# Fused attention and two MoE layers on one core: four of a slot's seven second-layer sums made by a ScalarE copy and an accumulating transfer

## Chip, cores and metric

The kernel runs on one core of a Trainium2 chip. The metric is device microseconds of one execution. One execution was also taken by the hardware profiler; all rows below come from it.

## The reference, cut to what matters

```python
# attention: 8 batches, 8 heads, 576 tokens, head size 64
kv = einsum('bhsd,bhse->bhde', k, v)
o  = einsum('bhsd,bhde->bhse', q, kv)
o  = o / sqrt(mean(o*o) + 1e-6) * g_norm          # -> x: 4608 tokens x 512
# first MoE layer (512 -> 2048 -> 512)
h = x @ w_in;  g = max(h, 0)**2;   x = g @ w_out
# second MoE layer (512 -> 2048 -> 512)
h = x @ w_in;  g = h * cos(h);     out = g @ w_out
```

All arrays are float32. A float32 product is made of three float32r matmuls on a high and a low part of each operand (high by high, high by low, low by high).

## The kernel before, in words

The 4608 tokens are worked in big tiles of 1024 tokens, in two halves of `ht` = 512; the last tile has 512 tokens, `ht` = 256. The part of the kernel that matters here walks 30 slots `(m, t, q)`: layer m, tile t, and a share q of the hidden units. The second layer (m = 1) has five tiles of four slots each, q = 0 to 3. A slot makes a 2 by 2 block product in two steps with seven block products each (Strassen's scheme in Winograd's form) in place of eight: `first_product` (x by w_in, into the PSUM tiles FA and FB), then a chain of ScalarE and VectorE operations for h*cos(h) (`cos_1` to `cos_5`) and block differences (`s_block`), then `second_product` (g by w_out, into the PSUM tiles SA and SB). The last slot of a tile, q = 3, makes its second step with `second` and `drain`, in the ordinary way, and stores the result to `out`.

The two steps are woven together on TensorE: while slot k makes its first products, the second products of slot k - 1.25 are issued between them. A product of the first step has 12 matmuls, one of the second step has 24 in a full tile (12 in the last tile). The time of one product of each is called a phase here; a slot has seven.

The second products come in the order `S_ORDER = (0, 2, 3, 4, 5, 1, 6)` and alternate between SA and SB. For four of them a product starts a bank anew or goes on adding in it, so each bank must have been read before the product after next begins. After the last matmul of a product `drain_product` reads the bank. The partial sums of a tile are four SBUF tiles of 128 x 1024 float32 (`sums`), kept over the tile's four slots. At q = 0 the products 0, 2, 3 and 6 start their sum with a ScalarE copy (L695); in all other cases VectorE adds the bank to the sum (L698).

`SUM_OF` says which sum a product goes to: 0 and 1 to (0,0), 2 and 5 to (1,1), 3 and 4 to (0,1), 6 to (1,0).

Weights come from DRAM, one transfer of 512 KB for each product (`load_wi`, L476, and `load_ws`, L481), issued on SP's queue. They share 16 buffers (`w_p`) with the four sums, so a load waits on SP until an earlier product has set a buffer free. `conv_p` is a pool of two buffers of 4 KB per partition with the tag "raw"; it serves the conversion of weights, which is over before the second products of the second layer begin. GpSimd's queue (POOL) issues no transfer in this part of the kernel; its only ones are 16 stores of 144 KB in the attention part (L354).

Each engine runs its instructions in the order in which they were issued.

Of the kernel before, what the change touches and what calls it, by code (L numbers as in the profile page):

```python
# [8 lines left out]
F32 = mybir.dt.float32  # L9
# [4 lines left out]
ALU = mybir.AluOpType  # L14
PSUM = bass.MemoryType.PSUM

P = 128
# [5 lines left out]
def kernel(  # L23
# [15 lines left out]
    nc = tc.nc  # L39
# [25 lines left out]
    conv_p = ctx.enter_context(tc.tile_pool(name="conv", bufs=2, side="left"))  # L65
# [356 lines left out]
    slots = [(m, t, q) for m in range(2) for t in range(len(TILES)) for q in groups_of[m]]  # L422
    ORDER = (0, 1, 3, 2, 5, 4, 6)
    W_OF = (0, 1, 3, 4, 6, 5, 2)
    BLOCKS = {(0, 0): 2, (1, 1): 5, (0, 1): 6, (1, 0): 7}
    S_ORDER = (0, 2, 3, 4, 5, 1, 6)
    xb, wi, wo, kept, hs, ys, sums, quads = {}, {}, {}, {}, {}, {}, {}, {}

    def big(pool, dtype, name, ht):
# [145 lines left out]
    def units(k):  # L575
        m, t, q = slots[k]
        half = TILES[t][1] // P if m else NKC
        return [(j, i) for j in (1, 0) for i in range(half)]
# [75 lines left out]
    def blocks_of(t, x, m=1):  # L654
        if m == 0:
            return x[:, :, :TILES[t][1]]
        return x.rearrange("p c n -> p (c n)").rearrange("p (b n) -> p b n", n=2 * P)[:, :TILES[t][1] // P]

    def s_bank(k, i):
        return psum[("SA", "SB")[(k + (i in (1, 2, 4))) % 2]]  # L660

    def second_product(k, i):
        m, t, q = slots[k]
        ps = blocks_of(t, s_bank(k, i), m)
        w, g = wo.pop((k, i)), gs.pop((k, i))
        nb = TILES[t][1] // P if m else 2
        for b in range(nb):
            n = 0
            for pp in range(2):
                for x, y in ((0, 0), (0, 1), (1, 0)):  # L670
                    if m == 0:
                        lhs, rhs = w[:, x, pp, b, :], g[y][:, pp, :]
                    else:
                        lhs, rhs = g[y][:, pp, b * P:(b + 1) * P], w[:, x, pp, :, :].rearrange("p i n -> p (i n)")
                    nc.tensor.matmul(  # L675
                        ps[:, b, :],
                        lhs,
                        rhs,
                        start=(i in (0, 1, 2) and n == 0 and (m == 0 or b % 2 == 0)),
                        stop=(n == 5),  # L680
                        skip_group_check=True,
                    )
                    n += 1
                    if n == 6 and b == nb - 1:
                        drain_product(k, i)
                    yield
# [3 lines left out]
    def drain_product(k, i):  # L690
        m, t, q = slots[k]
        ps, (d, j) = blocks_of(t, s_bank(k, i), m), SUM_OF[i]
        if q == 0 and m and i in (0, 2, 3, 6):
            sums[m, t, d, j] = e = w_p.tile([P, 2, 512], F32, tag="w", name="sum")
            nc.scalar.copy(out=blocks_of(t, e), in_=ps)  # L695
        else:
            e = blocks_of(t, sums[m, t, d, j], m)
            nc.vector.tensor_tensor(out=e, in0=ps, in1=e, op=ALU.add)  # L698


    chunks = [(t, f) for t in range(NTILE) for f in range(NH)]
# [5 lines left out]
    def at(n, fn, *a):  # L707
        jobs.append((n, len(jobs), fn, a))

    def pos(slot):  # L710
        return nA0 + slot + 0.002
# [67 lines left out]
    for k, (m, t, q) in enumerate(slots):  # L779
# [7 lines left out]
        if (m, q) in seven:  # L787
            for f, i in enumerate(S_ORDER):
                at(pos(k + LAG2 + (f - 2.7) * PH), load_ws, k, i)
# [54 lines left out]
    def run_slots():  # L844
# [9 lines left out]
            for k in range(len(slots))  # L854
            for i in (S_ORDER if slots[k][0::2] in seven else range(len(units(k)) // 4))
        ]
# [99 lines left out]
```

## Time and profile before

| | |
|---|---|
| median of 3 runs | 1594.78 us |
| lowest, highest | 1592.71, 1594.97 us |
| the profiled execution | 1593.87 us |
| its span, first to last instruction | 1592.1 us |
| TensorE busy, share of the span | 1555.1 us, 98% |
| VectorE busy | 1273.3 us, 80% |
| ScalarE busy | 992.7 us, 62% |
| GpSimd busy | 60.8 us, 4% |
| mean granted TensorE clock | 0.994 |

Times in the rows are microseconds from the start of the span. PE is TensorE's matmuls, PEld its weight loads, DVE VectorE, ACT ScalarE, POOL GpSimd, SP SyncE; a q behind a name is the engine's own instruction queue. L698 is line 698 of the kernel. "sum<-SA,sum" names the tile written and the tiles read.

### The profile page before, as it was taken

What the parts mean: (1) busy time and instruction counts of PE and PEld (TensorE: products, weight loads), DVE (VectorE), ACT (ScalarE), POOL (GpSimd) and SP (SyncE); (2) the same over time, 40 slices, a digit from 0 to 9 for tenths busy, and PEclk for the clock granted to TensorE, in tenths of its full rate; (3) what the DMA queues carried; (4) which work ended last, traced back from release to release, by engine and by line L of the source; (5) the groups of instructions that cost most, each with busy time, mean ns of one, the idle gap of its engine ahead of it and who ended that gap; (6) DMA issues with size and microseconds to landing.
All of it is one profiled execution on the core that took longest, in us unless ns stands there. A gap on an engine that the chain in (4) does not pass through costs nothing.

```text
span 1592.1 us, 23679 instructions
## 1 busy us (share of the span) xinstructions
PE 1555.1 (98%) x8840; PEld 1322.0 (83%) x8840; DVE 1273.3 (80%) x1724; ACT 992.7 (62%) x1422; POOL 60.8 (4%) x58
## 2 busy tenths in 40 slices
PE   5999999999999999999999999999999999999998
PEld 4777777778887778888888899889988998899897
DVE  7967767787766898989867789868986898689786
ACT  5977767784434666556646666666666666666664
POOL 1100112111100000000000000000000000000000
PEclk8999999999999999999999999999999999999999
DMA  9855876665568989898988856565656565656684
GB/s 316 279 168 159 256 238 223 200 207 184 164 214 274 318 283 352 304 353 292 351 311 333 286 177 212 180 244 172 212 187 237 172 213 180 229 174 206 214 338 191
DMA packets 214545, 382.20 MB, mean 240 GB/s; under 512 B 17312, under 2 KB 140704, under 8 KB 214432
## 3 DMA queue, kind: packets, MB, share of 16 engines
q1 hardware_dynamic: 213664, 378.34, 71.0%
q0 software_dynamic: 768, 2.36, 0.4%
q8 instruction: 70, 1.15, 0.3%
q14 instruction: 43, 0.35, 0.1%
HBM read 301.99 MB, written 78.64 MB: 239 GB/s over the span
## 4 chain that ended last, share of the span: by engine, by line
PE 87%; DVE 6%; DMA 3%; ACT 3%; issue 1%; SPq 0%; POOL 0%; DVEq 0%; ACTq 0%
PE FA L502 15%; PE FB L502 15%; PE SA L675 11%; PE SB L675 10%; PE acc L415 10%; PE l L378 8%; PE SA L604 6%; PE SB L604 6%; PE o L378 1%; PE ss L378 1%; DMA q<-in_qT 1%; PE o L257 1%; DMA x_d<-xo 1%; PE l L257 0%; DVE raw L173 0%
## 5 line engine op out<-in xcount | busy, mean ns | idle before, releaser
L502 PE MATMUL FA<-xh,wi 128*128 128x512 f32 (+1 forms) x840 | 304.0, 371 | 4.7 <-DVE h L526 1.7
L502 PE MATMUL FB<-xh,wi 128*128 128x512 f32 (+1 forms) x840 | 301.7, 369 | 0.0
L675 PE MATMUL SA<-ws,gh 128*128 128x256 f32 x792 | 197.0, 280 | 0.0
L675 PE MATMUL SB<-ws,gh 128*128 128x256 f32 x720 | 180.1, 280 | 0.0
L502 PEld LDWEIGHTS FA<-xh,wi 128*128 128x128 f32 x840 | 158.3, 189 | 20.8 <-DVE h L526 2.1
L502 PEld LDWEIGHTS FB<-xh,wi 128*128 128x128 f32 x840 | 157.7, 188 | 13.5
L675 PEld LDWEIGHTS SA<-ws,gh 128*128 128x128 f32 x792 | 147.8, 188 | 14.6 <-issue 0.2
L675 PEld LDWEIGHTS SB<-ws,gh 128*128 128x128 f32 x720 | 134.8, 188 | 13.6
L561 DVE SCALAR_TENSOR_TENSOR y<-y,h 128x1024 f32<-128x1024 f32 (+1 forms) x80 | 89.2, 1115 | 46.7 <-ACT y L557 46.7
L543 ACT ACTIVATE y<-h,zerob 128x1024 int32<-128x1024 f32 (+1 forms) x80 | 85.1, 1063 | 64.9 <-DVE h L522 64.9
L553 ACT ACTIVATE y<-y 128x1024 f32<-128x1024 f32 (+1 forms) x80 | 78.0, 976 | 75.8 <-DVE y L547 75.3
L415 PE MATMUL acc<-gh,wh 128*128 128x512 f32 x288 | 114.3, 398 | 0.0
L415 PE MATMUL acc<-gl,wh 128*128 128x512 f32 x288 | 113.5, 394 | 0.0
L415 PE MATMUL acc<-gh,wl 128*128 128x512 f32 x288 | 113.1, 393 | 0.0
L675 PE MATMUL SA<-ws,gl 128*128 128x256 f32 x396 | 111.0, 280 | 0.0
L502 PE MATMUL FB<-xl,wi 128*128 128x512 f32 (+1 forms) x300 | 110.9, 370 | 0.0
L502 PE MATMUL FA<-xl,wi 128*128 128x512 f32 (+1 forms) x300 | 110.8, 369 | 0.0
L652 DVE TENSOR_TENSOR gl<-y,gh 128x1024 fp32r<-128x1024 f32 (+1 forms) x75 | 83.5, 1114 | 30.0 <-ACT gh L651 30.0
L675 PE MATMUL SB<-ws,gl 128*128 128x256 f32 x360 | 100.9, 280 | 0.0
L378 PE MATMUL l<-xh,wh 128*128 128x512 f32 x240 | 96.5, 402 | 1.7 <-ACT xh L347 0.8
L378 PE MATMUL l<-xl,wh 128*128 128x512 f32 x240 | 94.9, 396 | 0.0
L378 PE MATMUL l<-xh,wl 128*128 128x512 f32 x240 | 94.4, 393 | 0.0
(190 smaller groups left out, 3859.8 us busy)
## 6 DMA issues: line engine op xcount, KB each, us to landing
wi<-wi_d SPq DMA_DIRECT2D x210, 512.0 KB, 5.1
ws<-ws_d SPq DMA_DIRECT2D x140, 512.0 KB, 5.3
wo<-wo_d SPq DMA_DIRECT2D x40, 512.0 KB, 5.2
kvld<-in_kv SPq DMA_DIRECT2D x32, 512.0 KB, 6.3
wi_d<-wh SPq DMA_DIRECT2D x24, 448.0 KB, 3.5
wi_d<-raw SPq DMA_DIRECT2D x24, 448.0 KB, 3.8
raw<-in_wA SPq DMA_DIRECT2D x20, 512.0 KB, 6.0
q<-in_qT SPq DMA_DIRECT2D x32, 288.0 KB, 4.0
```

Source lines behind the costliest of these rows:

```text
L257: nc.tensor.matmul(kv_ps[b][r, p, r], t[:n, 0, head], t[:n, 1, head], start=(c == 0 and p == 0), stop=(c == NSC - 1), skip_group_check=True,)
L378: nc.tensor.matmul(ps, a[:, 0, cs], m[:], start=(c == 0 and k == 0), stop=(c == NKC - 1 and k == 2))
L415: nc.tensor.matmul(o, a[:, cs], m[:], start=(f == 0 and n == 0), stop=(f == NH - 1 and n == 2), skip_group_check=True)
L502: nc.tensor.matmul(ps[:, pp, :], a, b, start=(i in (0, 1, 2) and n == 0), stop=(n == 5), skip_group_check=True)
L543: nc.scalar.activation(out=y.bitcast(I32), in_=hs[k, b], func=AF.Identity, bias=zerob)
L553: nc.scalar.activation(out=y, in_=y, func=AF.Sin, scale=math.pi)
L561: nc.vector.scalar_tensor_tensor(out=y, in0=y, scalar=-2.0 * math.pi, in1=hs.pop((k, b)), op0=ALU.add, op1=ALU.mult)
L604: nc.tensor.matmul(ps, lhs, rhs, start=(a == 0 and (x, y) == (0, 0)), stop=last, skip_group_check=True)
L652: nc.vector.tensor_tensor(out=l, in0=src, in1=as32(h), op=ALU.subtract)
L675: nc.tensor.matmul(ps[:, b, :], lhs, rhs, start=(i in (0, 1, 2) and n == 0 and (m == 0 or b % 2 == 0)), stop=(n == 5), skip_group_check=True,)
```

## The change

For the second layer, the four products 4, 5, 1 and 6 are no longer added to their sum by VectorE. ScalarE copies the bank to an SBUF tile `part` (a buffer of `conv_p`), and a transfer on GpSimd's queue adds `part` to the sum in SBUF. Where product 6 starts its sum (q = 0), its copy stays as it was. The first layer and the products 0, 2 and 3 are as before. The last condition (`k < len(slots) - 1`) is always true, since the last slot doesn't come here.

```diff
     S_ORDER = (0, 2, 3, 4, 5, 1, 6)
+    BY_DMA = (4, 5, 1, 6)
...
         else:
             e = blocks_of(t, sums[m, t, d, j], m)
-            nc.vector.tensor_tensor(out=e, in0=ps, in1=e, op=ALU.add)
+            if m and i in BY_DMA and k < len(slots) - 1:
+                part = blocks_of(t, conv_p.tile([P, 2, 512], F32, tag="raw", name="part"))
+                nc.scalar.copy(out=part, in_=ps)
+                nc.gpsimd.dma_start(out=e, in_=part, accum_op=ALU.add)
+            else:
+                nc.vector.tensor_tensor(out=e, in0=ps, in1=e, op=ALU.add)
```

## Rows read from the trace of the kernel before

**Rows 1.** The page, busy time of each engine, share of the span, instructions.
```profile
PE 1555.1 (98%) x8840; PEld 1322.0 (83%) x8840; DVE 1273.3 (80%) x1724; ACT 992.7 (62%) x1422; POOL 60.8 (4%) x58
```
**Rows 2.** Windows: stretch, length, then PE, PEld, DVE, ACT, POOL, clock, DMA, GB/s.
```profile
900.00:1592.00 692.00, 686.44 (x4239) 616.42 (x4237) 564.38 (x554) 434.75 (x474) 0.00 (x0) 1.00 0.62 211
...
1060.00:1100.00 40.00, 40.00 (x259) 36.33 (x258) 29.67 (x26) 26.88 (x28) 0.00 (x0) 1.00 0.65 224
1100.00:1150.00 50.00, 50.00 (x323) 45.36 (x322) 44.54 (x40) 32.26 (x33) 0.00 (x0) 1.00 0.65 207
...
1530.00:1540.00 10.00, 10.00 (x86) 10.00 (x85) 8.73 (x15) 7.28 (x13) 0.00 (x0) 1.00 1.03 418
...
1560.00:1570.00 10.00, 10.00 (x86) 10.00 (x85) 8.96 (x16) 6.38 (x11) 0.00 (x0) 1.00 0.83 335
1570.00:1580.00 10.00, 9.17 (x61) 8.28 (x61) 8.48 (x15) 7.68 (x13) 0.00 (x0) 1.00 0.00 0
```
**Rows 3.** Waits of PE from 900 to the end: total, times, longest.
```profile
PE SA L604 <- ACT y L557: 0.8, 1, 0.8
```
**Rows 4.** Lines 698 (first two) and 695, second layer: duration ns min/median/max, forms.
```profile
L698 DVE TENSOR_TENSOR sum<-SB,sum x45: 681/1217/1225, 917.1 to 1574.5; 128x1024 f32<-128x1024 f32 x36, 128x512 f32<-128x512 f32 x9
L698 DVE TENSOR_TENSOR sum<-SA,sum x40: 682/1217/1225, 922.8 to 1575.3; 128x1024 f32<-128x1024 f32 x32, 128x512 f32<-128x512 f32 x8
...
L695 ACT COPY sum<-SA x15: 578/1013/1017, 900.3 to 1537.8; 128x1024 f32<-128x1024 f32 x12, 128x512 f32<-128x512 f32 x3
```
**Rows 5.** Timeline, full tile, 1086 to 1093: start, length, engine, instruction.
```profile
1086.08 0.28 PE L675 MATMUL SB<-ws,gh 128*128 128x256 f32 x1
1086.20 0.28 PE L675 MATMUL SA<-ws,gh 128*128 128x256 f32 x1
...
1086.62 1.22 DVE L698 TENSOR_TENSOR sum<-SB,sum 128x1024 f32<-128x1024 f32 x1
...
1091.68 0.28 PE L675 MATMUL SA<-ws,gh 128*128 128x256 f32 x1
...
1091.80 0.28 PE L675 MATMUL SB<-ws,gh 128*128 128x256 f32 x1
...
1092.00 1.01 ACT L695 COPY sum<-SA 128x1024 f32<-128x1024 f32 x1
```
**Rows 6.** DMA: GpSimd's queue (packets, MB, share), one issue group, landing of POOL's stores.
```profile
q0 software_dynamic: 768, 2.36, 0.4%
...
x_d<-xo POOLq DMA_DIRECT2D x16, 144.0 KB, 5.3
...
DMA to landing us min/median/max: 2.0/5.3/7.6
```
**Rows 7.** Last tile: SP's ws issues, first matmul of a product, ws landing 1520 to 1570.
```profile
1551.78 0.32 SPq L481 DMA_DIRECT2D ws<-ws_d  x1
...
1554.66 0.32 SPq L481 DMA_DIRECT2D ws<-ws_d  x1
...
1569.10 0.29 PE L675 MATMUL SA<-ws,gh 128*128 128x256 f32 x1
...
DMA to landing us min/median/max: 5.7/7.7/9.8
```
**Rows 8.** Timeline of the end, by engine: DVE, ACT, PE.
```profile
1569.06 0.69 DVE L698 TENSOR_TENSOR sum<-SB,sum 128x512 f32<-128x512 f32 x1
...
1571.47 0.68 DVE L698 TENSOR_TENSOR sum<-SA,sum 128x512 f32<-128x512 f32 x1
...
1575.31 0.69 DVE L698 TENSOR_TENSOR sum<-SA,sum 128x512 f32<-128x512 f32 x1
...
1571.05 0.63 ACT L557 ACTIVATE y<-y 128x512 f32<-128x512 f32 x1
...
1575.15 0.61 ACT L557 ACTIVATE y<-y 128x512 f32<-128x512 f32 x1
...
1574.98 0.28 PE L675 MATMUL SA<-ws,gh 128*128 128x256 f32 x1
1576.10 0.47 PE L604 MATMUL SA<-wo,gh 128*128 128x512 f32 x1 [0.83 <-ACT y L557]
```

## Prediction

> **What bounds the kernel now.** I read the page first: TensorE is busy for 98% of the span, VectorE for 80%, ScalarE for 62% [rows 1]. The windows of the second layer come next, since only that stretch changes. From 900 us to the end TensorE is busy for 686.4 of 692 us [rows 2], and the list of waits has one single entry for its matmuls there, 0.8 us near the end [rows 3]. A busy matmul engine could still run slowly, so I compared the count of matmuls: 259 in a 40 us window with VectorE busy for 74%, 323 in a 50 us window with VectorE busy for 89% [rows 2]. That is 6.5 per us in both. The rate doesn't follow VectorE's load. In the last tile it is 86 narrow matmuls per 10 us whether the DMA engines are at 1.03 or at 0.83 [rows 2]. So the second layer is set by TensorE's own rate, and taking work from VectorE (82% busy there, 564.38 of 692) can give back almost nothing. What is left to ask is whether the new way of summing makes TensorE wait.
>
> **What is removed.** The second layer has 85 instructions on L698, 68 full and 17 of half size [rows 4]. Products 4, 5 and 1 go in all three slots q = 0 to 2 and product 6 in two of them: 11 per tile, 44 full and 11 half over five tiles. On VectorE that removes 44 x 1.217 + 11 x 0.682 = 61.0 us, by the median and the least duration of the row [rows 4]. VectorE falls from 82% to 73%. On the path this is worth nothing, because no matmul waits for VectorE, except at the end (below).
>
> **What is added on ScalarE.** 55 copies from PSUM to SBUF. The row for just this operation is L695: 1.013 us full, 0.578 us half [rows 4], so 44 x 1.013 + 11 x 0.578 = 50.9 us. ScalarE goes from 434.75 to 485.7 of 692 us, 63% to 70%. It has room, and the copy is a little shorter than the add. The order matters more. The copy stands in ScalarE's queue at the place where the product ends, and behind it wait the cosine chain and the reads of FA and FB. How late may it be? The product on SB issues its last matmul at 1086.08 and ends at 1086.36; SB is written again from 1091.80 [rows 5]. Of these 5.4 us the add took 0.26 us to start and 1.22 us to run. A ScalarE copy starts as promptly: SA ends at 1091.96 and its copy runs from 1092.00 [rows 5]. With 0.3 us to start and 1.0 us to run, 4.1 us are left before TensorE stands. I price it at nothing; cover is these 4.1 us, and each us beyond them would be paid by TensorE.
>
> **What is added on GpSimd's queue.** 55 accumulating transfers, 512 KB (256 KB in the last tile), SBUF to SBUF. No transfer of before accumulates, so the price is bounded. From below: a plain pass over the data. At the fullest the DMA engines move 418 GB/s [rows 2], so 512 KB take 1.25 us and 256 KB 0.63 us of all 16 engines. GpSimd's 16 stores agree within a sixth: 0.4% of 1592.1 us is 6.4 us for 2.36 MB, 370 GB/s [rows 6]. From above: reading the part, reading the sum and writing it as three full passes, 3.76 and 1.88 us. I take two passes, 2.5 and 1.25 us, since an add needs one operand more than a copy and the write of a plain pass is already in its price. Beside this stands a far upper bound, from the slowest landing of GpSimd's stores: 144 KB in 7.6 us [rows 6]. The Trainium skill, page "Collectives: The Full Stack", section "The bandwidth ceiling: the fold count and why AG ≠ RS ≠ AR", says that an add in the DMA engines costs the second read alone and not the adding; by that the sum would be the one below. No run here shows it yet.
>
> When must it land? Two buffers serve `part`, so the third copy of a slot waits for the first transfer. A phase is 5.6 us (SA starts at 1086.20, SB at 1091.80 [rows 5]). The copy ends 1.3 us after its product, the third is due two phases after the first: 11.2 + 0.3 - 1.3 = 10.2 us to land, and 14.3 us before TensorE waits (4.1 more). The same 10 us hold for the sum (0,0), which VectorE touches two phases after product 1. GpSimd's fastest store of 144 KB landed after 2.0 us [rows 6], of which 0.35 us is its pass at 418 GB/s; with two passes of 512 KB that is 2.0 - 0.35 + 2.5 = 4.2 us alone, and at most 2.5 more if it shares the engines with a load all the time: 4.2 to 6.7 us. Hidden. The engines bear it too: 0.65 of a slot's 39.2 us (seven phases) is 25.5 us of loads, plus 4 x 2.5 makes 35.5 us.
>
> **The last tile.** Here the phases halve but a load is still 512 KB, and the DMA engines are full (1.03, 418 GB/s from 1530 [rows 2]). SP issues a load each 2.88 us in each of two streams (1551.78, 1554.66 [rows 7]); two loads cost 2.5 us, so 0.37 us per phase is free. The load issued at 1554.66 serves the product that starts at 1569.10: a lead of 14.4 us, of which landing takes up to 9.8 us [rows 7]. The slack is 4.6 us. Of the 11 transfers seven fall into the full stretch: three from slot 26 (about 1529 to 1535), four from slot 27 (about 1549 to 1558). The first three take 3 x 1.25 = 3.8 us, less 7 phases x 0.37 = 2.6: 1.2 us of backlog. The next four add 5.0 and 4 phases give back 1.5: 4.7 us against 4.6 of slack. That is a stall of 0.1 us; I take 0.2.
>
> **The end.** The last four adds of slot 28 become copies; they start today at 1569.06, 1571.47 and, the last, at 1575.31 [rows 8]. TensorE's one wait ends at 1576.10, just after the last add frees SA (1575.31 + 0.69), and 48 matmuls follow. Product 6 ends at 1575.26 and its copy needs the buffer of product 5. That one's copy comes behind L557 (1571.05 [rows 8]), ends by 1572.3 and its transfer, 2.0 - 0.35 + 1.25 = 2.9 us on DMA engines that are idle by then (0.00 [rows 2]), lands at 1575.2: in time. But the copy may stand behind L557 on ScalarE (1575.15 to 1575.76), so SA is free at 1576.34 instead of 1576.00: +0.35. With the slowest landing, 7.6 us, it would be 1579.9 + 0.6, +4.5. A gain is possible too: two adds of 0.6 us leave VectorE's chain ahead of 1576, but the add that ends last is replaced by a copy that is only 0.1 us shorter. I take +0.5.
>
> **Sum.** 0 (full tiles) + 0.2 + 0.5 = +0.7 us. On the profiled execution: 1593.87 + 0.7 = 1594.6 us. The median of the runs shown lies 0.9 us above that execution, so for a median 1594.78 + 0.7 = 1595.5 us. A difference of 0.2%, 3.2 us, is about the least that a measurement of this kernel can tell from no change.
>
> **Rivals.** (A) Hidden, as summed: 1595.5, own range 1592.5 to 1598. Chance 0.63.
>
> (B) Slower by the last tile: a transfer costs so much engine time that the weight loads come late. It decides from about 1.25 us per 256 KB. At four passes (2.5 us) seven transfers take 17.5 us, less 4.1 free and 4.6 of slack: 8.8 us of stall, 1605. At three passes 4.4 us, 1600. For it: the engines are at 1.03 there. Against: the lead of 14.4 us. Chance 0.20.
>
> (C) Slower in every slot: landing takes over 14.3 us, the third copy stands in front of ScalarE's queue and TensorE waits for the bank. The far bound, (7.6 - 2.0) x 512/144 + 2.0 = 21.9 us, gives 7.6 us per slot; in the 12 full slots 91 us, 1687. At 18 us it is 12 x 3.7 = 44 us, 1640. Against: the fastest store, 2.0 us [rows 6]. The Trainium skill, page "SBUF — State Buffer", section "SBUF: two separate sides", speaks for it: descriptors of GpSimd's transfers are written by GpSimd and starve while VectorE runs an operation that takes both ports. By the same page two-input adds have no such mode, and VectorE's work in this stretch is two-input. Chance 0.12.
>
> (D) Faster by over 0.2%: only if TensorE's rate rose when VectorE is relieved, against the equal rates in [rows 2]; without that, all waits together are 0.8 us. 0.05, at about 1590.
>
> So faster 0.05, same 0.63, slower 0.32. The range reaches from 1591 (most of D left out) to 1611 (C and the far end of B left out).
>
> **What the profile would show.** Right: 55 ScalarE copies near 1.01 and 0.58 us, 30 adds left on L698 in the second layer, landing of the accumulating transfers of 4 to 7 us, DMA share in full tiles up from 0.65 to about 0.9, 6.5 matmuls per us as now. Wrong: PE or PEld waiting for wi or ws after 1530 (B); ScalarE copies waiting for a transfer and PE for ScalarE at each slot's sixth product (C); more matmuls per us (D).

## The result, and the profile after

The changed kernel takes 1612.68 us (median of 4 runs, 1612.33 to 1615.89) against 1594.7 us of the kernel before in 4 runs: 1.0116 times as long, interval 1.0102 to 1.0129. That is slower, and just above the range that was given. The profiled span grew from 1592.1 to 1610.6 us, by 18.5 us.

The page of the changed kernel: busy time by engine, GpSimd's queue (packets, MB, share of the 16 DMA engines' span) and the new transfers (KB each, us from issue to landing).

```profile
PE 1563.9 (97%) x8840; PEld 1326.6 (82%) x8840; DVE 1220.7 (76%) x1669; ACT 1035.1 (64%) x1477; POOL 107.9 (7%) x113
...
q0 software_dynamic: 8688, 28.32, 8.7%
...
sum<-part POOLq DMA_DIRECT2D x44, 512.0 KB, 7.5
```

Work moved as the diff says [rows 1]: VectorE is busy for 52.6 us less, ScalarE for 42.4 us more. The queue's share went from 0.4% [rows 6] to 8.7%: 140.1 - 6.4 = 133.7 us of all 16 engines for 44 full and 11 half transfers, 49.5 full ones in all, so 2.70 us for 512 KB.

The windows of two full-tile stretches, with the columns of [rows 2].

```profile
1060.00:1100.00 40.00, 40.00 (x259) 36.29 (x258) 26.67 (x23) 29.37 (x31) 2.54 (x3) 1.00 0.84 264
1100.00:1150.00 50.00, 48.15 (x310) 43.42 (x308) 37.86 (x34) 32.90 (x35) 3.39 (x4) 1.00 0.84 247
```

In the first, TensorE makes the same 259 matmuls as before, with VectorE busy for 26.67 instead of 29.67 us: nothing is given back. The DMA share rose from 0.65 to 0.84. In the second, TensorE stands for 1.85 us. The list of TensorE's matmul waits from 880 us to the end shows where it stands; before there was one, of 0.8 us [rows 3].

```profile
PE SA L676 <- issue: 6.1, 3, 2.3
PE SA L605 <- ACT part L701: 2.4, 1, 2.4
PE SB L676 <- issue: 1.7, 1, 1.7
PE SB L676 <- ACT part L701: 1.3, 1, 1.3
PE SA L676 <- ACT part L701: 1.0, 1, 1.0
PE FA L503 <- ACT m L517: 0.5, 1, 0.5
```

L701 is the new copy, L702 the transfer, L704 the addition that stays with VectorE. "issue" is time for which the profile shows no releaser; each such wait ends 0.1 us after an L704 addition on the same bank, so it is VectorE's late reading of that bank. No matmul waits for wi or ws.

When the finished sums of a tile are stored tells in which tile the time is lost. First three stores of the kernel before, then the same of the changed one (start, issue time, queue): the second group of stores of the first full tile, of the fourth, and the last of all.

```profile
1053.49 0.99 SPq L842 DMA_DIRECT2D out<-sum  x2
...
1518.07 0.99 SPq L842 DMA_DIRECT2D out<-sum  x2
...
1586.67 2.33 SPq L842 DMA_DIRECT2D out<-sum  x4
```

```profile
1053.67 0.99 SPq L849 DMA_DIRECT2D out<-sum  x2
...
1525.18 0.99 SPq L849 DMA_DIRECT2D out<-sum  x2
...
1605.13 2.33 SPq L849 DMA_DIRECT2D out<-sum  x4
```

The lag is 0.2 us after the first tile, 7.1 after the fourth and 18.5 at the end. So there are two losses: 6.9 us in the full tiles, 11.4 us in the short last tile and behind it.

**The loss in the full tiles.** The chain of waits from 1125 to 1150, changed kernel:

```profile
1127.92 12.86 DMA xraw<-y_d
...
1140.80 0.04 DVE xraw L453
...
1143.16 1.14 DVE sum L704
```

And the timeline there (start, length, instruction, in brackets the idle time before it and what ended it):

```profile
1140.80 1.23 DVE L453 TENSOR_TENSOR xraw<-xraw 128x1024 f32<-128x1024 f32 x1 [3.90 <-DMA xraw<-y_d]
...
1143.08 1.22 DVE L704 TENSOR_TENSOR sum<-SA,sum 128x1024 f32<-128x1024 f32 x1
...
1144.40 0.36 PE L676 MATMUL SA<-ws,gh 128*128 128x256 f32 x1 [1.85 <-issue]
```

At a tile's start SP loads the next tile's x quarters (`xraw<-y_d`). One of them lands 12.86 us after its issue. VectorE stands 3.90 us before a subtraction that needs it (L453, x block 5), the addition that empties SA is queued behind, and TensorE stands 1.85 us for SA. At 1302.78 the same happens, with 4.35 us on VectorE and 2.31 us on TensorE. Why was this subtraction no trouble before? The two rows below give the lines' first and last start, of the kernel before and then of the changed one.

```profile
L452 DVE TENSOR_TENSOR xraw<-xraw x2: 1217/1218/1219, 1169.5 to 1328.0; 128x1024 f32<-128x1024 f32 x2
```

```profile
L453 DVE TENSOR_TENSOR xraw<-xraw x2: 1225/1228/1230, 1140.8 to 1302.8; 128x1024 f32<-128x1024 f32 x2
```

Each engine's order is fixed when the kernel is built, by a planner, and need not be that of the program text. With four additions per slot gone from VectorE it moved the subtraction ahead: 29 instructions behind the block's first subtraction before, with six of VectorE's additions between, and 4 behind it now, with none between, counted in VectorE's own order. The diff doesn't touch that line. (These are the places at the starts of the second to the fourth tile.)

The lost time includes a lower clock. Windows of the changed kernel behind the 2.31 us wait, and at the end:

```profile
1304.00:1308.00 4.00, 1.69 (x11) 1.47 (x10) 4.00 (x5) 0.56 (x1) 0.00 (x0) 0.96 0.91 353
1308.00:1312.00 4.00, 4.00 (x18) 3.62 (x18) 4.00 (x5) 2.68 (x4) 0.00 (x0) 0.61 0.48 150
...
1592.00:1596.00 4.00, 3.06 (x10) 2.48 (x11) 2.41 (x4) 2.67 (x5) 1.26 (x2) 0.80 0.72 131
1596.00:1600.00 4.00, 4.00 (x15) 3.17 (x15) 0.19 (x1) 0.00 (x0) 0.00 (x0) 0.78 0.00 0
```

A granted clock of 0.61 is a window spent mostly at the lower level (1.2 of 2.4 GHz): 18 matmuls in it where other windows have 28, and 0.39 x 4 = 1.6 us lost. Waits of 1.85 and 2.31 us, the 0.5 us for `m` and 1.6 us of clock are 6.3 of the 6.9 us.

**The loss in the last tile.** Its waits, changed kernel, timeline of ScalarE, TensorE and VectorE:

```profile
1569.28 0.59 ACT L701 COPY part<-SA 128x512 f32<-128x512 f32 x1 [2.74 <-DMA sum<-part]
...
1569.92 0.39 PE L676 MATMUL SA<-ws,gh 128*128 128x256 f32 x1 [0.96 <-ACT part L701]
...
1577.33 0.69 DVE L704 TENSOR_TENSOR sum<-SA,sum 128x512 f32<-128x512 f32 x1 [2.81 <-DMA sum<-part]
...
1578.12 0.36 PE L676 MATMUL SA<-ws,gh 128*128 128x256 f32 x1 [1.93 <-issue]
```

The accumulating transfers' landings from 1540 to 1600, and a window of that stretch with the columns of [rows 2], where the DMA engines are full (1.05):

```profile
DMA to landing us min/median/max: 3.2/7.1/8.5
...
1560.00:1570.00 10.00, 9.04 (x76) 8.84 (x75) 5.66 (x9) 6.30 (x13) 1.70 (x2) 1.00 1.05 370
```

A phase of this tile is 2.88 us [rows 7]. By the prediction's own working for the full tiles the third copy of a slot wants its buffer back after 2 x 2.88 + 0.3 - 0.9 = 5.2 us; the transfers take 7.1 and up to 8.5. So the copy stands 2.74 us in front of ScalarE's queue, and TensorE stands behind it. The next slot's product 0 goes to the same quarter (0,0) as product 1, and its addition on VectorE stands 2.81 us for product 1's transfer. Each of the two comes twice in this tile (3.50 us at 1545.21, and 2.67 us at 1553.20; for the latter the profile names no releaser, but product 1's transfer, issued at 1546.08, lands after 7.0 us, at 1553.1). At the end TensorE waits for the copy of product 6:

```profile
1590.69 0.58 ACT L701 COPY part<-SB 128x512 f32<-128x512 f32 x1
1591.15 0.73 ACT L544 ACTIVATE y<-h,zerob 128x512 int32<-128x512 f32 x1
1591.78 0.61 ACT L568 CAST gh<-y 128x512 fp32r<-128x512 f32 x1
1592.31 0.58 ACT L701 COPY part<-SA 128x512 f32<-128x512 f32 x1
...
1592.94 0.50 PE L605 MATMUL SA<-wo,gh 128*128 128x512 f32 x1 [2.38 <-ACT part L701]
```

TensorE's product is done at 1590.56, but ScalarE first copies product 1 and takes a step of the cosine chain and a cast. The five waits add 1.93 + 1.7 + 1.3 + 1.0 + (2.4 - 0.8) = 7.5 us, the lower clock behind the last one (0.20 + 0.22) x 4 = 1.7 us: 9.2 of 11.4 us. I have no row for the rest; the first matmuls behind a wait come more slowly than later ones (four take 0.89 us from 1554.00 instead of 0.48).

### The profile page after: what moved, and what is told of

Read it like the earlier page. It is cut to its first block, busy times and chain, and to the rows that moved or that the text cites. A ratio compares the mean times of both kernels' runs of the same rounds, so it can differ in the third digit from the quotient of the medians.

```text
span 1610.6 us, 23887 instructions
## 1 busy us (share of the span) xinstructions
PE 1563.9 (97%) x8840; PEld 1326.6 (82%) x8840; DVE 1220.7 (76%) x1669; ACT 1035.1 (64%) x1477; POOL 107.9 (7%) x113
## 3 DMA queue, kind: packets, MB, share of 16 engines
q0 software_dynamic: 8688, 28.32, 8.7%
## 4 chain that ended last, share of the span: by engine, by line
PE 81%; DVE 7%; DMA 5%; ACT 4%; issue 2%; SPq 1%; POOL 0%; DVEq 0%; POOLq 0%; ACTq 0%
PE FA L503 14%; PE FB L503 14%; PE SA L676 10%; PE acc L415 10%; PE SB L676 8%; PE l L378 8%; PE SA L605 6%; PE SB L605 6%; PE o L378 1%; PE ss L378 1%; DMA xraw<-y_d 1%; DMA xraw<-x_d 1%; DMA ws<-ws_d 1%; DVE gl L653 1%; DMA q<-in_qT 1%
## 5 line engine op out<-in xcount | busy, mean ns | idle before, releaser
L702 POOL DMA_DIRECT2D sum<-part x55 | 46.7, 850 | 1138.9 <-ACT part L701 1113.5
L548 DVE SCALAR_TENSOR_TENSOR y<-y,h 128x1024 f32<-128x1024 int32 (+1 forms) x80 | 89.0, 1112 | 12.8 <-ACT y L544 12.5
```

What stands on the lines that cost most here:

```text
L548: nc.vector.scalar_tensor_tensor(out=y, in0=y.bitcast(I32), scalar=-1.0, in1=hs[k, b], op0=ALU.mult, op1=ALU.add)
L702: nc.gpsimd.dma_start(out=e, in_=part, accum_op=ALU.add)
```

## The experiments

Each ratio is to runs of the kernel before on the same chip (medians 1594.58, 1593.63 and 1593.72 us), with its 95% interval.

**Two places or one cause?** The condition at L699 limits the transfers to the full tiles (44 of them), or to the last tile (11).

```diff
-            if m and i in BY_DMA and k < len(slots) - 1:
+            if m and i in BY_DMA and t < len(TILES) - 1:      # e1;  e2: t == len(TILES) - 1
```

Full tiles only: 

> The new sums only in the four full tiles (44 transfers); in the last tile VectorE adds as before. Theory A (two separate losses: at the starts of the third and fourth tile VectorE stands at the subtraction for block product 5 until its x transfer has landed, and the bank behind it is read late; in the last tile copies wait for a part buffer and adds for a transfer): the loss of the full tiles alone, 7.2 us of the 18.5, so about 1602 us, with TensorE waits of about 2 us near 1144 and 1306 and none after 1500. Theory B (the weight loads of the last tile come late because the DMA engines are full, and this is the main loss): about 1595 to 1597. Theory C (each ScalarE copy costs a little everywhere): 44 of 55 parts of 18.5, 1609.

Measured 1603.5 us, 1.0059 (1.0042 to 1.0075). Its waits of TensorE behind VectorE, and VectorE's for the x loads, both from 880 us to the end:

```profile
PE SA L676 <- issue: 5.1, 3, 2.1
...
DVE xraw L453 <- DMA xraw<-y_d: 12.5, 4, 4.2
```

TensorE's three waits come at 987, 1149 and 1309 us (1.81, 2.12 and 1.14 us). So it also waits at the start of the second tile, where the changed kernel doesn't, and the granted clock stays at 1.00 behind all three.

Last tile only: 

> The new sums only in the last tile (11 transfers). Theory A: the loss of the last tile alone, 11.2 us, so about 1606, with five TensorE waits after 1520 of 1 to 2.4 us, each behind a copy that waits for a part buffer or an add that waits for a transfer. Theory B: 1606 as well, but with waits for wi or ws. Theory C: 1598.

Measured 1606.3 us, 1.0079 (1.006 to 1.0097), with the five waits of the changed kernel's last tile (2.4, 2.0, 1.9, 1.5, 1.2 us) and ScalarE's for a buffer:

```profile
ACT part L701 <- DMA sum<-part: 6.7, 2, 3.7
```

Each place costs by itself: 0.59% and 0.79%, together 1.38% against 1.16% for both at once, within the width of the intervals.

**The order on VectorE.** The transfers stay in the full tiles only, and the subtraction is kept behind the last addition that VectorE makes before it, by a dependency of order alone (no data, no semaphore). It then stands 24 places behind the block's first subtraction, with three of VectorE's additions between.

```diff
+            sub = nc.vector.tensor_tensor(out=out, in0=x, in1=y, op=ALU.subtract)
+            if m and i == 5 and drains:
+                tc.add_manual_dep(sub.ins, drains[-1].ins.name, order_only, reason="behind the drain")
...
+                drains.append(nc.vector.tensor_tensor(out=e, in0=ps, in1=e, op=ALU.add))
```

> As the run with the full tiles alone, and the subtraction for block product 5 of a new tile is kept behind the last VectorE add that was issued before it, so that it stands about 20 rows later in VectorE's order, near its place in the kernel before. Transfers, copies and buffers are the same. Theory A: the waits near 1144 and 1306 go, 1595 (between 1593 and 1597). Rival (the x transfer is late by itself and whoever reads it next stalls, wherever it stands): 1601 to 1603 as without it.

Measured 1593.72 us, 0.9998 (0.9989 to 1.0008): the whole loss of the full tiles is gone. TensorE's only wait, and the landings of `xraw` from 1080 to 1460:

```profile
PE SA L609 <- ACT y L562: 0.8, 1, 0.8
...
DMA to landing us min/median/max: 3.3/8.5/14.0
```

The loads land as late as in the changed kernel (3.2/8.3/13.3) and later than before (3.3/5.7/7.7), but neither VectorE nor TensorE stands for them.

**What the last tile waits for.** Transfers in the last tile only, with four buffers for `part` instead of two.

```diff
+                if t == len(TILES) - 1:
+                    part = temp([P, 512], F32, "part").rearrange("p (b n) -> p b n", n=2 * P)
...
```

> As the run with the last tile alone, with four buffers for part there in place of two. Theory A: the copies no longer wait; the waits of 1.3, 1.0 and 2.4 us and the clock that falls after the last go, the two waits of VectorE for the transfer of product 1 stay: 1599 to 1601. Theory B (full DMA engines): the transfers are as many, so about 1606, unchanged.

Measured 1601.89 us, 1.0041 (1.0023 to 1.0059), just above the forecast and with a wide spread (1596.25 to 1605.44; the profiled execution is the slowest). The waits for a buffer are gone on ScalarE and TensorE. I had expected the 2.4 us at the end and the lower clock behind them to go too; both stay, so that wait is not for a buffer. Left besides is VectorE's late reading of the bank, and here the granted clock falls to 0.66 behind TensorE's wait of 1.8 us:

```profile
PE SA L605 <- ACT part L704: 2.4, 1, 2.4
PE SB L676 <- issue: 1.8, 1, 1.8
...
1548.00:1552.00 4.00, 3.92 (x21) 3.72 (x22) 3.54 (x6) 2.77 (x5) 0.00 (x0) 0.66 1.02 416
```

Next, four buffers, and in the last tile product 1 goes back to VectorE (`BY_DMA = (4, 5, 6)`): 

> Only the last tile's sums are changed, with four buffers for the copies, and product 1 goes back to a VectorE addition (8 transfers). Theory A (in the last tile the copies wait for a buffer, and the next slot's product-0 addition waits for the transfer of product 1 into the same quarter of the sum): with both gone the VectorE waits at the sum line fall from 4.35 and 0.66 us to nothing and the TensorE waits of 1.8 and 0.7 us go with them; what stays is the wait of 2.4 us for the copy of product 6 near the end and the lower clock behind it. 1596 to 1599 us. Theory B (transfers in the last tile make the loads late, whatever product they serve): three fewer of eleven transfers, so about a quarter less loss than with four buffers, 1600 us, with waits on loads.

Measured 1594.18 us, 1.001 (1.0001 to 1.0018). VectorE's waits at the sum line for transfers are gone, as theory A has it. But so is most of the 2.4 us at the end, which I had expected to stay. TensorE's one wait, and ScalarE's timeline at the last copy:

```profile
PE SA L605 <- ACT part L704: 0.9, 1, 0.9
...
1576.18 0.60 ACT L568 CAST gh<-y 128x512 fp32r<-128x512 f32 x1
1576.69 0.58 ACT L704 COPY part<-SA 128x512 f32<-128x512 f32 x1
```

With one copy less in ScalarE's queue the copy of product 6 starts 0.3 us after its product's last matmul (1576.09 + 0.28) instead of 1.75 us. The end was held by two copies close together, not by one.

Then product 6 of the last slot with products goes back to VectorE too (`and (k, i) != (len(slots) - 2, 6)`): 

> As the run with four buffers and product 1 on VectorE, and product 6 of the last slot with products also goes back to VectorE (7 transfers). Theory A (the wait of 2.4 us at the end is the copy of product 6, which stands in ScalarE's queue behind the casts of the last slot): that wait falls to the 0.8 us of the kernel before, the granted clock stays at 1.00 as long as there, 1594 to 1596 us. Theory B (transfers in the last tile cost by themselves): 1599 us.

Measured 1594.82 us, 1.0013 (1.0004 to 1.0022): no better than with that copy. TensorE's wait at the end is now 2.0 us, not 0.8: VectorE's addition starts at 1575.91, behind a subtraction of the last slot. The time agrees with the forecast; the reason that I gave for it doesn't.

**The price of adding.** All 55 transfers write the copy over the sum instead of adding it (`accum_op` left out, so the sums are not formed): 

> All 55 transfers write the copy over the quarter of the sum instead of adding it; the sums are left out, everything else and VectorE's order stay as in the changed kernel. If an accumulating transfer takes two passes on the DMA engines, the POOL queue falls from 8.7% of the DMA engines' span to 4.4 to 5%, the landings and with them the x loads come sooner, and a part of the loss goes: 1600 to 1608 us, with the same places of waiting. If accumulation costs no more than a plain copy, the queue stays near 8.7% and the time at 1612 us.

Measured 1598.82 us, 1.0034 (1.0024 to 1.0044), a little below the forecast. GpSimd's queue, and the issue times on GpSimd (ns):

```profile
q0 software_dynamic: 7984, 28.32, 4.4%
...
L702 POOL DMA_DIRECT2D sum<-part x55: 527/528/562, 916.7 to 1578.6; - x55
```

4.4% of 1595.9 us less the 6.4 us of the other stores is 63.8 us, 1.29 us for 512 KB. Adding costs 2.1 times a plain pass, with the same 28.32 MB on the queue's row. The Trainium skill, page "Collectives: The Full Stack", section "The bandwidth ceiling: the fold count and why AG ≠ RS ≠ AR", says that a reduction reads twice what a copy reads. The trace agrees in the price, on transfers between SBUF and SBUF; the second read itself stands in no row. The planner's early order is the same as in the changed kernel (4 places, no addition between), but the x loads now land in 8.7 us at most, and none of TensorE's waits of 1.85 and 2.31 us is there. So the early order costs nothing when the loads are prompt, and the late loads cost nothing when what reads them stands behind the additions (the run with the order kept): the loss of the full tiles needs both. The 2.4 us at the end, the only wait of TensorE over 0.6 us, and the lower clock behind it stay.

**No transfer at all.** ScalarE makes the 55 copies and VectorE adds each to its sum: 

> ScalarE makes the 55 copies, and VectorE adds each copy to the sum; no transfer. Theory A (the loss comes from the transfers' landings and from what stands behind them on VectorE): no VectorE wait on an x load above 2 us, and 1594 to 1597 us. Theory C (the copies on ScalarE by themselves hold TensorE up, as ScalarE reads the bank later than VectorE did): TensorE waits on the copies all over, 1602 us or more; the one wait of 2.4 us at the end, which stands behind a copy, stays by both.

Measured 1596.08 us, 1.0021 (1.0011 to 1.003). The only wait of TensorE:

```profile
PE SA L605 <- ACT part L701: 2.6, 1, 2.6
```

The copies on ScalarE are hidden in every slot but at the end. There the wait is 1.8 us longer than before, and the granted clock behind it (0.67 and 0.90 in the two windows of 4 us from 1576) costs another 1.7 us: together that covers the whole 0.21%.

**Are the two losses separate?** All 55 transfers, with the order kept: 

> All 55 transfers, and on VectorE the subtraction for x block 5 kept behind the last drain that VectorE makes, in every tile. Theory A (two separate losses): the full tiles' waits of 2 us behind the x loads go, the last tile's five waits stay, 1604 to 1607 us. Theory B (one loss, the transfers' traffic, which only moves to another place): 1610 us or more, with waits at other places in the full tiles.

Measured 1605.77 us, 1.0081 (1.0067 to 1.0095), the loss of the last tile alone. From 880 to 1500 us TensorE waits for nothing; among its five waits in the last tile are the two behind VectorE:

```profile
PE SA L680 <- issue: 2.0, 1, 2.0
PE SB L680 <- issue: 1.8, 1, 1.8
```

And both mends together, 44 transfers in the full tiles and seven in the last: 

> The 44 transfers of the full tiles with that order kept, and seven of the last tile's eleven with four buffers (product 1 and the last product 6 go back to VectorE). Theory A: nothing waits over 1 us on TensorE but the one wait at the end, the time is that of the kernel before within 0.2%, 1592 to 1597 us, and no faster, although VectorE is busy some 55 us less. Theory B: 1600 us or more. If TensorE gained from a less busy VectorE it would show here: under 1591 us.

Measured 1595.83 us, 1.0016 (1.0007 to 1.0025). The page's busy line, and TensorE's one wait:

```profile
PE 1557.3 (98%) x8840; PEld 1323.8 (83%) x8840; DVE 1223.9 (77%) x1673; ACT 1031.7 (65%) x1473; POOL 102.9 (6%) x109
...
PE SA L609 <- ACT y L558: 2.0, 1, 2.0
```

VectorE is busy 49.4 us less than before [rows 1] and the time is not shorter. No version that was run beats the kernel before by what can be told apart.

## Why the prediction was wrong, step by step

**What bounds the kernel: right.** TensorE's rate is unchanged with a less busy VectorE (259 matmuls in 40 us in both), and the mended kernel shows that 49.4 us off VectorE buy nothing. Rival D is out.

**What is removed and added: right in kind and in the price of one.** 30 additions stay on L704 in the second layer; the copies take 1.01 and 0.58 us as read from [rows 4]. VectorE's busy time fell by 52.6 us and not 61.0, and ScalarE's rose by 42.4 and not 50.9. The prediction added up durations, and neighbouring instructions overlap in the record: three of VectorE's of 1.22 us start at 1303.92, 1305.06 and 1306.19. That the copies are hidden held in all slots (no wait without the transfers) but not at the end.

**The transfer's price: right.** Two passes, 2.5 us, were taken; 2.70 us was measured. Its landing was too low: 4.2 to 6.7 us for a full transfer, 7.5 us by the page, 10.2 at most. In the full tiles that was still hidden behind the 10.2 us that the prediction had worked out: no copy waited there.

**"When must it land?": the step that failed first.** The limit was worked out for phases of 5.6 us alone. In the last tile it is 5.2 us, and half-size transfers landed after 7.0 to 8.5 us, as they share DMA engines that are full (1.04 and over); the last four, when the loads were over, landed after 3.2 us. The prediction looked in that tile only for what the transfers do to the loads, and set 0.2 us. Rival C had this mechanism (the third copy in front of ScalarE's queue, TensorE behind it), but put at 14.3 us and in every slot; it came in the slots of the last tile alone. Of the held-up descriptors that rival C weighed nothing is seen in the issues: all 55 on GpSimd take 0.84 to 0.91 us. With four buffers and product 1 on VectorE the loss of that tile falls from 0.79% to 0.10%.

**"The last tile", loads late (rival B): not seen.** No matmul waited for wi or ws, in any run with transfers there. The loads do land later. The ws loads issued from 1520 to 1575 in the changed kernel, against 5.7/7.7/9.8 before [rows 7]:

```profile
DMA to landing us min/median/max: 6.7/10.1/13.2
```

But if each load is matched with its product by their order, none of the wi and ws loads there lands less than 2.5 us before its product's first matmul. The least was 2.5 us in the kernel before too, not the 4.6 us that the prediction took.

**"The end": mis-sized.** +0.5 us was taken, for one copy behind L557. The wait grew by 1.6 us, and a clock lower for two windows took another 1.7. Two copies and two instructions of the chain stand in ScalarE's queue there.

**What was left out.** The prediction asked when TensorE's loads come, not the x loads at a tile's start, and took the order of the untouched instructions as given. The planner's new order and the later x loads together made the 0.59% of the full tiles; with either one undone (the order kept, or plain copies) TensorE's waits are gone.

**What stays open.** Some 0.6 us of the full tiles' loss and 2.2 us of the last tile's have no row. Why the mended kernel and those close to it lie 0.10 to 0.16% above the kernel before isn't settled beyond the waits of 0.9 and 2.0 us at the end.

## What to carry to other kernels

Work out a buffer's limit for the shortest phase in the program, not for the commonest one: with half the tile the time for a transfer to land fell from 10.2 to 5.2 us, while the landing itself, on full DMA engines, only fell from 7.5 to 7.1 us (medians). If instructions are taken out of a queue that a planner orders, compare the order of all that is left there, above all of those that wait for transfers: an untouched subtraction, 4 instead of 29 places behind its neighbour, had a part in about a third of the loss here (1.16% with it, 0.81% with the order kept). Work moved off an engine that nothing waits for gave nothing back here, and every new link (a buffer, a transfer onto a sum that is read two phases later, one more queue) is a place where something can wait.

## What the runs showed of the hardware that I had not expected

An accumulating transfer between SBUF tiles takes the DMA engines for 2.70 us per 512 KB and a plain one for 1.29 us, though the queue's row counts the same 28.32 MB for both; its issue takes GpSimd 0.85 us instead of 0.53 us. With the DMA share at 0.84 in the windows from 1060 to 1150, single x loads still took 12.9 to 14.0 us to land. A wait of TensorE can cost more than its row: after 2.31 us of idle time the granted clock fell to 0.61 in a window of 4 us, after 2.38 us to 0.80 and 0.78 in two, and in the run with four buffers after 1.8 us to 0.66. After 1.85 and 1.93 us in the changed kernel it stayed at 1.00, so the length of one wait doesn't tell whether the clock falls.
